# A fused attention, routing, experts and feed-forward kernel: attention loads run three groups ahead instead of eight, its two kinds of units alternate, and its rows are stored as they come

## The chip, the core and the metric

The kernel runs as one program on one NeuronCore of a Trainium2 chip. The metric is the time of one execution on the device, in microseconds; shorter is better. Five instruction streams run beside each other and wait for one another through semaphores: TensorE (PE; its weight loads are shown as PEld), VectorE (DVE), ScalarE (ACT), GpSimd (POOL) and SyncE (SP). SP computes nothing here: its stream issues DMAs. POOL issues DMAs too, besides some work of its own. All DMAs share the core's 16 DMA engines.

## What is computed

Attention over four batches, eight heads, 576 tokens and 64 features, in float32. Heads 0 to 3 see the last 32 tokens; heads 4 to 7 see the earlier tokens of the same residue modulo 32. The rows are then the input of a top-1 mixture of eight experts, and its result that of a feed-forward block with a squared ReLU:

```python
rel = pos[:, None] - pos[None, :]
mask_local = (rel >= 0) & (rel < stride)
mask_strided = (rel >= 0) & (pos[None, :] % stride == pos[:, None] % stride)
masks = np.stack([mask_local if h < H // 2 else mask_strided for h in range(H)], axis=0)
scores = np.where(masks[None], scale * (q @ k.transpose(0, 1, 3, 2)), -1e9)
attn = softmax(scores);  x = rows_of(attn @ v)              # (2304, 512)
...
logits = x @ w_gate + modality_bias[modality_id]
e_idx = np.argmax(logits, axis=1)                           # one expert a row
out[mask] = gate_w[mask, None] * (np.maximum(x[mask] @ w1[e], 0.0) @ w2[e])
...
r = np.maximum(x @ w_in, 0.0)
return (r * r) @ w_out
```

## The kernel before

**Stages.** `attention_and_routing` computes attention, stores its rows `xn` in the DRAM tensor `x1`, and works out which rows go to which expert. `moe_and_ffn` then gathers rows from `x1` by expert (the gathers wait for all stores), multiplies them by the experts' weights, and goes on to the feed-forward block. The change lies in the first stage alone.

**Units.** The list `units` holds 40 units of work: 22 strided ones (`"s"`, 108 rows each) and 18 local ones (`"l"`, 128 rows each). Before, all strided units come first (units 0 to 21), then all local ones (22 to 39). One turn of the loop over `k` is a software pipeline: SP gets the loads and stores of this turn; PE computes the scores of unit k into `sp` (L207), transposes the result of unit k-5 (`xq`, L317) and the weights of unit k-2 (`pp`, L236), and multiplies the weights of unit k-3 by v into `xp` (L253 for strided, L264 for local units). DVE takes the maximum, subtracts, and normalises unit k-5 into `xn`; ACT does the exponential and the copies out of PSUM. For every pair of rows' tiles that is complete (two local units, and the strided units that hold the same tokens), turns also carry the products with the gate's weights (`xq`, L358) and, a turn later, a short fold (`sp`, L369). `KEEP0` and `KEEP` add small matmuls on zeros (L192): four to two a turn in the first eleven turns, then one a strided unit and none a local one.

**Loads.** Units are loaded in groups: four of one strided unit, nine of two strided units, nine of two local units. A group has a tile `qk` and a tile `v`; each comes from a ring of `NLD` buffers, so a load waits until the group that held its buffer before has been used up (scores for `qk`, the product with v for `v`). `loads_to` issues them in order on SP; at turn k it goes as far as the group of unit k plus `NLD` - 1. Here `NLD` is 9. SP is in order: a load that waits holds up all DMAs behind it. It also waits, before each DMA, for the eighth one before it to land.

**Stores.** `store` writes one unit's `xn`: a local one as one DMA on SP (L302), a strided one as two or three on POOL (L310). `xn` has a ring of `NXN` = 15 buffers. Stores begin at turn `ST0` = 12, and those of local units wait until all loads have been issued.

**Other names.** `wg` and `fold` are the gate's weights and a small constant, loaded on SP (L403, L404) just ahead of the first load of a group of two. `N_LOC` is the number of tiles whose softmax of logits is done inside the loop. Line numbers here and in the rows are those of the kernel before.

Of the kernel before, what the change touches and what calls it, by code (L numbers as in the profile page):

```python
# [19 lines left out]
NE, FF, F2 = 8, 1024, 2048  # L20
STRIDE = 32
NJ = S // STRIDE
NTL = NT // 128
# [7 lines left out]
NST = -(-NT // SU)  # L31
# [9 lines left out]
NCV = 4  # L41
XR = 4
KEEP_R = (7, 9, 9)
NXN = 15
ST0 = 12
KEEP_D = 2
KEEP_X = 5
EARLY0 = (0, 0)
# [3 lines left out]
KEEP = {"s": 1, "l": 0}  # L52
KEEP0 = {0: 0, 1: 4, 2: 4, 3: 4, 4: 4, 5: 4, 6: 3, 7: 3, 8: 3, 9: 2, 10: 2}
NWM = 4
NLD = 9
NWS = 3
N_LOC = 8


@with_exitstack  # L60
# [25 lines left out]
def attention_and_routing(es, tc, a, x1, res):  # L86
    nc = tc.nc
    sy, ac, ve, gp, pe = nc.sync, nc.scalar, nc.vector, nc.gpsimd, nc.tensor
# [3 lines left out]
    cst = es.enter_context(tc.tile_pool(name="a_cst", bufs=1))  # L92
    ld = es.enter_context(tc.tile_pool(name="a_ld", bufs=NLD))
    wk = es.enter_context(tc.tile_pool(name="a_wk", bufs=3))
# [22 lines left out]
    wg = cst.tile([128, 4, 32], F32, name="wg")  # L117
    fold = cst.tile([128, NE], F32, name="fold")
# [4 lines left out]
    rt.warm = warm  # L123
    rt.spare = lambda: (bank("a0"), bank("a1"))

    units = [("s", t) for t in range(NST)] + [("l", t) for t in range(NTL)]
    NU = len(units)
    groups, gof = [], {}
    for kind, sizes in (("s", (1, 1, 1, 1) + (2,) * 9), ("l", (2,) * 9)):
# [29 lines left out]
    ngl = [0]  # L159

    def loads_to(k):
        while ngl[0] <= min(k, len(groups)):
            gi = ngl[0]
            if gi < len(groups):
                load_qk(gi)
            if gi > 0:
                load_v(gi - 1)
            ngl[0] += 1

    def geom(k):  # L170
        kind, t = units[k]
        gi, o = gof[kind, t]
        if kind == "s":
            return kind, t, 128 if t < NST - 1 else 64, 64, gi, o
        return kind, t, 128, 64, gi, o
# [6 lines left out]
    def stage_s(k):  # L182
        kind, t, n, w, gi, o = geom(k)
        sp = ps.tile([128, 2, 512], F32, tag="sp", name="sp")
        qk = qk_t[gi]
        if kind == "s":
            mk = mstr
        else:
            mk = mloc[:, 1 if (2 * t) % 9 == 0 else (2 if (2 * t + 1) % 9 == 0 else 0), :]
        mk = mk.unsqueeze(1).to_broadcast([128, 2, w])  # L190
        for i in range(KEEP0.get(k, KEEP[kind])):
            pe.matmul(sp[:, i % 2, 256:512], lhsT=warm[:, 0:128], rhs=warm[:, 0:256], start=True, stop=True)  # L192
        for par in range(2):
            pe.matmul(sp[:, par, 0:2 * w].rearrange("p (b w) -> p b w", b=2),
                      lhsT=identb, rhs=mk, start=True, stop=False, skip_group_check=True)
        for pr in range(2):
            for par in range(2):
                r0 = 64 * par
                if kind == "s":
                    cq, ck = (4 * o + pr) * SU, (4 * o + 2 + pr) * SU  # L200
                    blocks = [(g, cq + g * SR, m, ck + g * SR, m) for g, m in sgroups(t)]
                else:
                    cq, ck = 256 * pr + 128 * o, 512 + (256 + QB) * pr + 128 * o
                    blocks = [(j / 2, cq + QB * j, QB, ck + QB * j, 2 * QB) for j in range(4)]
                for g, cq, m, ck, mk_ in blocks:
                    p0 = int(64 * g)
                    pe.matmul(  # L207
                        sp[p0:p0 + m, par, pr * w:pr * w + mk_],
                        lhsT=qk[r0:r0 + 64, cq:cq + m],
                        rhs=qk[r0:r0 + 64, ck:ck + mk_],  # L210
                        start=False, stop=True, skip_group_check=True,
                    )
        st[k, "s"] = sp[0:n, :, 0:2 * w].rearrange("p a (b w) -> p a b w", b=2)
        return sp

    def v_max(k):
        kind, t, n, w, gi, o = geom(k)
        mx = wk.tile([128, 2, 2], F32, tag="mx", name="mx")
        ve.tensor_reduce(out=mx[0:n], in_=st[k, "s"], axis=AX.X, op=ALU.max)
        st[k, "m"] = mx  # L220

    def v_sub(k):
        kind, t, n, w, gi, o = geom(k)
        sm = wk.tile([128, 4 * w], F32, tag="sm", name="sm")
        sm4 = sm.rearrange("p (a b w) -> p a b w", a=2, b=2)[0:n]
        ve.tensor_tensor(out=sm4, in0=st.pop((k, "s")),
                         in1=st.pop((k, "m"))[0:n].unsqueeze(3).to_broadcast([n, 2, 2, w]), op=ALU.subtract)
        ac.activation(out=sm[0:n], in_=sm[0:n], func=AF.Exp, scale=scale)
        st[k, "p"] = sm

    def stage_t(k, pp=None):
        kind, t, n, w, gi, o = geom(k)
        p = st.pop((k, "p"))
        pp = bank("pp") if pp is None else pp
        for i in range(2):
            pe.transpose(pp[:, 128 * i:128 * i + n], p[0:n, 128 * i:128 * i + 128], ident[0:n, 0:n])  # L236
        pt = wk.tile([128, 2, 128], F32, tag="pt", name="pt")
        ac.activation(out=pt[:, :, 0:n], in_=pp.rearrange("p (h n) -> p h n", n=128)[:, 0:2, 0:n], func=AF.Copy)
        st[k, "t"] = pt
# [40 lines left out]
    def v_norm3(k):  # L280
        kind, t, n, w, gi, o = geom(k)
        xn = wk.tile([128, 256], F32, tag="xn", name="xn", bufs=NXN)
        ve.tensor_tensor(
# [12 lines left out]
    stores = []  # L296

    def store():
        k, xn = stores.pop(0)
        kind, t = geom(k)[0:2]  # L300
        if kind == "l":
            sy.dma_start(out=x1[t * 128:t * 128 + 128, 0:256], in_=xn)  # L302
        else:
            for g, rows in sgroups(t):
                c, p = 2 * t * CT + g * CT, 64 * g
                end = p + rows
                while p < end:
                    m = min((end - p) // NJ, STRIDE - c % STRIDE)
                    dst = x1.rearrange("(b j r) f -> b r j f", j=NJ, r=STRIDE)[c // STRIDE, c % STRIDE:c % STRIDE + m]
                    gp.dma_start(out=dst[:, :, 256:512], in_=xn[p:p + m * NJ])  # L310
                    c, p = c + m, p + m * NJ
# [54 lines left out]
    def folds(p, dst):  # L366
        t0, t1, lt = p
        for i in range(t1 - t0):
            pe.matmul(dst[:, NE * i:NE * i + NE], lhsT=lt[:, 128 * i:128 * i + 128], rhs=fold, start=True, stop=True)  # L369
        return t0, t1, dst[:, 0:NE * (t1 - t0)]  # L370
# [3 lines left out]
    def add(p):  # L374
        rt.add(*p)
        n_add[0] = p[1]

    def features(k):

        xq = bank("xq")  # L380
        t0 = lg_done[0]
        t1 = min(t0 + 2, lg_ready(max(0, k)))
        if t1 > t0 + 1:
            products(t0, t1, xq[:, 256:512])
        stage_x(k, xq)
        if t1 > t0 + 1:
            lt_p.append(fetch(t0, t1, xq[:, 256:512]))
            lg_done[0] = t1
# [11 lines left out]
    ngl[0] = 2  # L400
    loads_to(3)
    sy.dma_start(out=mloc, in_=a["mloc"])
    sy.dma_start(out=wg[:, :, 0:NE], in_=a["w_gate"].rearrange("(c p) e -> p c e", p=128))  # L403
    sy.dma_start(out=fold, in_=a["fold"])  # L404
    ac.activation(out=sc1, in_=sc1, func=AF.Exp)
    wu = bank("xp")
    for i in range(9):
# [5 lines left out]
    def side(n):  # L413
        while n and todo:
            if next(todo[0], todo) is todo:
                todo.pop(0)
            else:
                n -= 1

    def norm(u):  # L420
        v_norm1(u)
        v_norm2(u)
        v_norm3(u)

    loc = 0
    for k in range(NU):
        if k >= LN:
            norm(k - LN)
        side(1)
        loads_to(geom(k)[4] + NLD - 1)  # L430
        for _ in range(2):
            if k >= ST0 and len(stores) > 1 and (units[stores[0][0]][0] == "s" or ngl[0] > len(groups)):
                store()
        sp = stage_s(k)
        fd = folds(lt_p.pop(0), sp[:, 0, 192:256]) if lt_p else None
        v_max(k)
        if fd:
            add(fd)
        side(1)
        if k >= LX:  # L440
            features(k - LX)
        if k >= LT:
            stage_t(k - LT)
        side(1)
        v_sub(k)
        side(1)
        if k >= LV:
            stage_v(k - LV)
        if k == 3:
            rt.load_consts()  # L450
        if k == 8:
            rt.bias()
        if loc == 0 and n_add[0] >= N_LOC:
            todo += [rt.local(0, N_LOC), rt.gates(0, N_LOC)]
            loc = N_LOC

# [62 lines left out]
class Routing:  # L519
# [4 lines left out]
    def t_(self, shape, dt, name):  # L524
        return self.cst.tile(shape, dt, name=name)
# [88 lines left out]
    def finish(self):  # L614
# [19 lines left out]
        cb = t_([128, 2, 128], BF16, "cnb")  # L634
        gts = self.gates(N_LOC, T)
        next(gts)
# [1165 lines left out]
```

## Time and profile before

| | us |
|---|---|
| median of 3 runs (727.41 to 732.12) | 728.55 |
| the profiled execution | 728.09 |
| its span, first to last instruction | 726.3 |
| PE busy in the span | 702.6 (97%) |
| DVE, ACT, POOL busy | 516.6, 407.0, 151.6 |

The profiled execution lies 0.46 us under the median. A row of the span's slices has 40 digits, each the busy share of 18.2 us in tenths; PEclk is the clock that was granted to TensorE in the same tenths. The chain of waits runs backwards from the last instruction, at each step to what released it; "issue" in it is time in which the engine waited for nothing that the profile shows. The DMA queue called "instruction" carries the program itself to the engines, q1 carries what SP issues, q0 what POOL issues.

### The profile page before, as it was taken

To read this page: it belongs to the slowest core of one execution; us is meant where nothing else is said; L and a number is where in the kernel's file an instruction comes from. 1 tells how busy PE (TensorE), PEld (TensorE's weight loads), DVE (VectorE), ACT (ScalarE), POOL (GpSimd) and SP (SyncE) were. 2 spreads that over 40 slices of the span, in tenths; PEclk is the share of its full clock that TensorE was granted. 3 is DMA by queue.
4 is the path that set the end of the run, shared out by engine and by line. 5 is a ranking of instruction groups with operands and counts; after the bars stand their busy time and mean duration, and the time that the engine had idled before them with its cause. 6 is when DMAs were issued, how large, how long until landed. Compare 5 with 4: busy or idle time off the path is not lost.

```text
span 726.3 us, 15653 instructions
## 1 busy us (share of the span) xinstructions
PE 702.6 (97%) x6012; PEld 653.0 (90%) x6012; DVE 516.6 (71%) x1021; ACT 407.0 (56%) x791; POOL 151.6 (21%) x215
## 2 busy tenths in 40 slices
PE   8898997999999999999999999999999999999995
PEld 5665656999999989999999999999999999999995
DVE  5667776678868778775567899847747796773784
ACT  3455445545565466544566776657627746663761
POOL 7651013102320241021002444540000004000004
PEclk9879999999999999999999999999999999999998
DMA  8994118557686598455145799998887879878832
GB/s 257 390 382 156 59 39 264 202 191 230 232 288 196 175 312 304 159 176 216 38 163 166 272 333 357 366 323 256 250 247 247 256 234 328 254 247 245 258 90 88
DMA packets 69422, 167.90 MB, mean 231 GB/s; under 512 B 11064, under 2 KB 14552, under 8 KB 69344
## 3 DMA queue, kind: packets, MB, share of 16 engines
q1 hardware_dynamic: 53312, 125.14, 53.5%
q0 software_dynamic: 16032, 41.73, 16.0%
q8 instruction: 49, 0.80, 0.5%
q14 instruction: 29, 0.24, 0.1%
HBM read 128.00 MB, written 38.80 MB: 230 GB/s over the span
## 4 chain that ended last, share of the span: by engine, by line
PE 91%; DMA 2%; issue 2%; DVE 2%; POOL 1%; ACT 1%; SPq 0%; another core or an unknown queue 0%; POOLq 0%; ACTq 0%; DVEq 0%
PE hp L878 14%; PE yp L889 14%; PE fhp L1154 9%; PE op L1175 9%; PE lb L1472 7%; PE mb L1545 7%; PE md L1472 5%; PE la L1472 5%; PE md L1545 4%; PE ma L1545 4%; PE sp L207 2%; PE xq L317 2%; PE xp L253 1%; PE pp L236 1%; POOL out_dram L1182 1%
## 5 line engine op out<-in xcount | busy, mean ns | idle before, releaser
L848 DVE TENSOR_TENSOR w<-stg,w 128x1024 fp32r<-128x1024 f32 x56 | 68.4, 1223 | 43.1 <-ACT w L844 43.0
L844 ACT ACTIVATE w<-stg 128x1024 fp32r<-128x1024 f32 x56 | 59.2, 1059 | 70.3 <-PE yp L889 45.3
L878 PE MATMUL hp<-xh,w 128*128 128x384 f32 (+1 forms) x448 | 92.4, 328 | 1.9 <-ACT xh L870 0.7
L878 PEld LDWEIGHTS hp<-xh,w 128*128 128x128 f32 x448 | 76.7, 188 | 3.8 <-ACT w L844 1.3
L889 PE MATMUL yp<-hh,w 128*128 128x384 f32 x384 | 76.2, 340 | 0.0
L1154 PE MATMUL fhp<-xh,w 128*128 128x384 f32 x256 | 70.5, 336 | 0.0
L889 PEld LDWEIGHTS yp<-hh,w 128*128 128x128 f32 x384 | 66.9, 188 | 0.0
L1182 POOL DMA_INDIRECT out_dram<-x2t,idn x12 | 14.0, 1168 | 220.2 <-DVE x2t L1447 218.3
L1472 PE MATMUL lb<-xh,ws 128*128 128x384 f32 x192 | 55.0, 337 | 0.0
L1200 POOL DMA_DIRECT2D wd<-w x48 | 34.4, 897 | 88.5 <-DVE w L999 85.5
L1175 PE MATMUL op<-w,gh 128*128 128x512 f32 x192 | 49.1, 391 | 0.0
L1521 DVE TENSOR_TENSOR gl<-g,gh 128x384 fp32r<-128x384 f32 x64 | 33.5, 556 | 21.0 <-ACT gh L1520 21.0
L1154 PEld LDWEIGHTS fhp<-xh,w 128*128 128x128 f32 x256 | 46.7, 188 | 1.2
L878 PE MATMUL hp<-xl,w 128*128 128x384 f32 (+1 forms) x224 | 46.3, 328 | 0.0
L1154 PE MATMUL fhp<-xl,w 128*128 128x384 f32 x128 | 43.2, 338 | 0.0
L881 ACT ACTIVATE hh<-hp 128x384 fp32r<-128x384 f32 (+1 forms) x56 | 25.5, 456 | 31.1 <-PE hp L878 30.7
L1450 ACT ACTIVATE g<-g 128x384 f32<-128x384 f32 x48 | 25.1, 522 | 32.0 <-DVE g L1447 31.8
L1520 ACT ACTIVATE gh<-g 128x384 fp32r<-128x384 f32 x64 | 32.6, 523 | 16.4 <-PE mb L1545 8.2
L889 PE MATMUL yp<-hl,w 128*128 128x384 f32 x192 | 41.1, 336 | 0.0
L1175 PEld LDWEIGHTS op<-w,gh 128*128 128x128 f32 x192 | 35.6, 188 | 5.4
L878 PEld LDWEIGHTS hp<-xl,w 128*128 128x128 f32 x224 | 39.1, 188 | 0.0
L1545 PE MATMUL mb<-ws,gh 128*128 128x256 f32 x264 | 38.6, 282 | 0.5 <-ACT gh L1520 0.5
(299 smaller groups left out, 1723.1 us busy)
## 6 DMA issues: line engine op xcount, KB each, us to landing
ws<-wd SPq DMA_DIRECT2D x112, 512.0 KB, 4.5
stg<-in_wcat_dram SPq DMA_DIRECT2D x56, 512.0 KB, 4.0
stg<-in_w2cat_dram SPq DMA_DIRECT2D x32, 512.0 KB, 5.3
wd<-w POOLq DMA_DIRECT2D x48, 256.0 KB, 6.1
wd<-co POOLq DMA_DIRECT2D x16, 512.0 KB, 4.1
wd<-co POOLq DMA_DIRECT2D x32, 256.0 KB, 5.1
qk<-in_qkl_dram SPq DMA_DIRECT2D x9, 544.0 KB, 9.7
v<-in_vl_dram SPq DMA_DIRECT2D x9, 528.0 KB, 8.2
```

The costliest lines, as they stand in the source:

```text
L844: ac.activation(out=w[:, 0, :], in_=t, func=AF.Copy)
L848: ve.tensor_tensor(out=w[:, 1, :], in0=t, in1=w[:, 0, :].bitcast(F32), op=ALU.subtract)
L878: pe.matmul(hp, lhsT=w[:, wi, 128 * k:128 * k + 128], rhs=x[:, k, 0:n], start=(i == 0), stop=(i == 11))
L881: ac.activation(out=hh, in_=hp, func=AF.Relu)
L889: pe.matmul(yp[c][:, 0:SLOT], lhsT=w[:, wi, 512 + 128 * c:640 + 128 * c], rhs=x, start=(j == 0 and x is hh and wi == 0), stop=(j == NC1 - ...
L1154: pe.matmul(hp, lhsT=w[:, v, 128 * k:128 * k + 128], rhs=xs[ch, k // 2][xv][:, k % 2, :], start=(i == 0), stop=(i == 11))
L1175: pe.matmul(ops[ch][t], lhsT=x[:, 128 * t:128 * t + 128], rhs=w[:, v, :], start=(j == ORD[0] and first), stop=(j == ORD[-1] and last))
L1200: gp.dma_start(out=wd[lay, p // 4, 7 * (p % 4) + unit[lay][i]], in_=src)
L1472: pe.matmul(M[m], lhsT=w[:, v, k, :], rhs=xp_c[c][x][xv][:, k, :], start=(i < 3 and n == 0), stop=(n == 5), skip_group_check=True)
L1520: ac.activation(out=gh, in_=src, func=AF.Copy)
L1521: ve.tensor_tensor(out=gl, in0=src, in1=gh.bitcast(F32), op=ALU.subtract)
L1545: pe.matmul(at[t], lhsT=x[:, 128 * t:128 * t + 128], rhs=w[:, v], start=(new and e == 0 and x is gh and v == 0 and first), stop=(e == 3 an ...
```

## The change

Four constants and the list of units are changed. The list now has ten strided units, then local and strided ones by turns (`l0 s10 s11 l1 s12 l2 s13 l3 ...`, with two strided units in a row once), then the last seven local ones. Groups are sorted by their first unit as before, so groups of local and strided units also come by turns. `NLD` is 4: loads run three groups ahead. A store is issued as soon as a second one is pending, whatever its kind. `wg` and `fold` are loaded on POOL, in turn 3 behind the constants of the routing. `NXN` is 12, `N_LOC` 10.

```diff
-NXN = 15
-ST0 = 12
+NXN = 12
+S_FIRST = 10
+L_LAST = 7
...
-NLD = 9
+NLD = 4
...
-N_LOC = 8
+N_LOC = 10
...
-    units = [("s", t) for t in range(NST)] + [("l", t) for t in range(NTL)]
+    units = [("s", t) for t in range(S_FIRST)]
+    ns, nl = S_FIRST, 0
+    while ns < NST or nl < NTL - L_LAST:
+        if nl < NTL - L_LAST and (ns == NST or nl * (NST - S_FIRST) <= (ns - S_FIRST) * (NTL - L_LAST)):
+            units.append(("l", nl))
+            nl += 1
+        else:
+            units.append(("s", ns))
+            ns += 1
+    units += [("l", t) for t in range(nl, NTL)]
...
-    sy.dma_start(out=wg[:, :, 0:NE], in_=a["w_gate"].rearrange("(c p) e -> p c e", p=128))
-    sy.dma_start(out=fold, in_=a["fold"])
...
-            if k >= ST0 and len(stores) > 1 and (units[stores[0][0]][0] == "s" or ngl[0] > len(groups)):
+            if len(stores) > 1:
                 store()
...
         if k == 3:
             rt.load_consts()
+            gp.dma_start(out=wg[:, :, 0:NE], in_=a["w_gate"].rearrange("(c p) e -> p c e", p=128))
+            gp.dma_start(out=fold, in_=a["fold"])
```

SP's stream at the start, before; 128x432 is the `qk` of one strided unit, 128x864 that of a group of two:

```order
L154 DMA v<-in_vs_dram 128x264
L402 DMA mloc<-in_mloc_dram 128x192
L403 DMA wg<-in_w_gate_dram 128x4x8
L404 DMA fold<-in_fold_dram 128x8
L144 DMA qk<-in_qks_dram 128x864
L154 DMA v<-in_vs_dram 128x264
L144 DMA qk<-in_qks_dram 128x864
```

The same place in the change:

```order
L164 DMA v<-in_vs_dram 128x264
L412 DMA mloc<-in_mloc_dram 128x192
L154 DMA qk<-in_qks_dram 128x864
L164 DMA v<-in_vs_dram 128x264
L154 DMA qk<-in_qks_dram 128x864
```

Two DMAs ahead of the first load of a group of two have moved to POOL.

SP's stream late in the loads, before:

```order
L156 DMA v<-in_vl_dram 128x1056
L146 DMA qk<-in_qkl_dram 128x1088
L156 DMA v<-in_vl_dram 128x1056 x2
L302 DMA x_60<-xn 128x256 x18
L1006 TENSOR_LOAD regs
```

Late in the loads of the change:

```order
L156 DMA qk<-in_qkl_dram 128x1088
L164 DMA v<-in_vs_dram 128x528
L154 DMA qk<-in_qks_dram 128x864
L166 DMA v<-in_vl_dram 128x1056
L312 DMA x_60<-xn 128x256
L156 DMA qk<-in_qkl_dram 128x1088
L164 DMA v<-in_vs_dram 128x528
L312 DMA x_60<-xn 128x256
```

The 18 stores of local units, which stood behind all loads, now stand between loads, and loads of strided (`qks`, `vs`) and local groups (`qkl`, `vl`) alternate.

PE's stream in the middle of the stage, before, one turn:

```order
L207 MATMUL sp<-qk 54x54 x8
L317 MATMUL xq<-ident,xn 128x128 x2
L236 MATMUL pp<-ident,sm 128x128 x2
L253 MATMUL xp<-v,pt 64x65 x8
L192 LDWEIGHTS warm
L192 MATMUL sp<-warm 128x256
```

In the change, the score and value products of three turns in the middle:

```order
L217 MATMUL sp<-qk 32x64 x16
L327 MATMUL xq<-ident,xn 128x128 x2
L246 MATMUL pp<-ident,sm 128x128 x2
L263 MATMUL xp<-v,pt 64x65 x8
L202 LDWEIGHTS warm
L202 MATMUL sp<-warm 128x256
...
L217 MATMUL sp<-qk 54x54 x8
L327 MATMUL xq<-ident,xn 128x128 x2
L246 MATMUL pp<-ident,sm 128x128 x2
L274 MATMUL xp<-v,pt 32x65 x16
...
L217 MATMUL sp<-qk 32x64 x16
```

A local unit has twice as many score and value products (x16) as a strided one (x8); turns of both kinds now alternate, where ten strided turns and then eighteen local ones stood. PE has the same instructions in all but one more small matmul on zeros.

## Rows read from the trace of the kernel before

**Rows 1.** The page: TensorE's granted clock in 40 slices of 18.2 us.

```profile
PEclk9879999999999999999999999999999999999998
```

**Rows 2.** Windows of the attention stage: busy time by engine, granted clock, DMA share, GB/s.

```profile
10.00:57.00 47.00, 41.70 (x854) 30.53 (x852) 32.08 (x104) 22.55 (x84) 28.46 (x51) 0.85 1.04 376
57.00:90.00 33.00, 30.07 (x1086) 20.10 (x1084) 23.82 (x88) 16.81 (x52) 1.73 (x3) 1.00 0.28 91
```

**Rows 3.** Chain of waits, attention stage: start, duration, what; PE pieces begin a turn's scores.

```profile
6.96 5.09 DMA qk<-in_qks_dram
12.10 0.42 PE sp L207 x16
...
22.52 0.34 issue
...
25.40 0.35 PE sp L207 x16
...
27.06 0.35 PE sp L207 x16
...
28.37 1.90 issue
...
46.40 0.35 PE sp L207 x16
...
51.53 1.08 issue
...
57.04 0.39 issue
...
59.56 0.38 PE sp L207 x32
...
60.84 0.38 issue
...
61.79 0.39 PE sp L207 x32
...
63.37 0.38 PE sp L207 x32
64.57 0.57 issue
...
80.01 0.32 issue
...
84.22 0.50 issue
```

**Rows 4.** A fine window behind the longest stall; columns as in rows 2.

```profile
32.00:34.00 2.00, 2.00 (x37) 1.52 (x34) 1.43 (x5) 0.80 (x4) 1.45 (x3) 0.50 1.04 391
```

**Rows 5.** PE's waits, 4 to 100 us: total us, times, longest us.

```profile
PE xp L253 <- issue: 2.6, 3, 1.9
PE sp L207 <- DMA qk<-in_qks_dram: 2.0, 1, 2.0
PE sp L207 <- issue: 2.0, 3, 1.1
PE xp L264 <- issue: 1.7, 4, 0.6
```

**Rows 6.** DMA at 27 to 29 us: packets, MB, share; issues, KB, us to landing.

```profile
q8 instruction: 1, 0.02, 3.4%
...
qk<-in_qkl_dram SPq DMA_DIRECT2D x1, 544.0 KB, 10.5
```

**Rows 7.** The same at 46 to 51 us.

```profile
qk<-in_qkl_dram SPq DMA_DIRECT2D x2, 544.0 KB, 7.6
```

**Rows 8.** The same at 58 to 62 us.

```profile
q8 instruction: 1, 0.02, 1.8%
...
v<-in_vl_dram SPq DMA_DIRECT2D x1, 528.0 KB, 5.0
```

**Rows 9.** SP's timeline at the start: start us, duration, DMA.

```profile
5.99 0.38 SPq L403 DMA_DIRECT2D wg<-in_w_gate_dram  x1
```

## The prediction, made before the change had run

> **What bounds the kernel now.** I began with the granted clock in slices [rows 1]. It stands at 9 nearly throughout; the two low digits, 8 and 7, cover 18 to 54 us, inside the attention stage. The reader is to see that the only stretch in which TensorE is slowed lies where the change is made. Windows split the stage [rows 2]: up to 57 us the DMA engines are full (share 1.04, 376 GB/s) and the clock averages 0.85; from 57 to 90 us the share is 0.28 and the clock is whole. PE is busy for 89% and 91% of the two, so the stage is a string of turns on PE, and whatever lengthens a turn lengthens the kernel.
>
> The chain of waits then shows the turns as starts of score products [rows 3]. A strided turn at full clock takes 27.06 - 25.40 = 1.66 us, a local one 63.37 - 61.79 = 1.58. Between them stand pieces named "issue", in which PE waited for nothing that the profile shows: 0.34, 1.90 and 1.08 us while the DMA engines are full, 0.3 to 0.6 us later. Ten such waits make 2.6 + 2.0 + 1.7 = 6.3 us [rows 5]. They come at regular distances. From the end of one to the end of the next it is 65.14 - 61.22 = 3.92 us and 84.72 - 80.33 = 4.39 us in the quiet part, and 30.27 - 22.86 = 7.41 us in the full one [rows 3]. I read them as PE having run out of program: a packet of the instruction queue moves just before such a wait ends, and it takes as long when DMA is full (3.4% of 16 engines over 2 us, 1.1 us) as when it is quiet (1.8% over 4 us, 1.15 us) [rows 6, 8]. So what grows is the time before the packet starts. It grows with the depth of the queue: loads take 10.5 us to land where the refill took 7.4, 7.6 us ahead of the wait at 51.5, and 5.0 us where the refill takes 3.9 [rows 6 to 8].
>
> The longest wait costs twice. After it the clock is 0.50, the lower of the two levels (1.2 GHz) [rows 4]. From 27.06 to 46.40 us seven strided turns ran in 19.34 us where seven at 1.66 make 11.62 [rows 3]. That is 7.7 us, the largest loss in the stage.
>
> **The change, part by part.**
>
> *Start.* PE waits 2.0 us for the load that was issued at 6.96 us and took 5.09 us to land [rows 3, 5]. Now the loads of `wg` and `fold` no longer stand ahead of it on SP; its slot is that of `wg`, 5.99 us [rows 9], 0.97 us earlier. Its new condition, that the scores of unit 0 are done so that their buffer is free, is met by then, since a turn's score products take 0.42 us and begin as soon as the first loads land. Those two loads are many small pieces and no longer move ahead of it either, so it may land sooner still. Bounds: 0.97 and the whole wait, 1.97; I take 1.5. On POOL the two loads stand before stores that have turns to spare, and nothing needs `wg` before turn 19.
>
> *Depth of the queue.* With four buffers, and from turn 10 on two groups in use at once, two groups at most are on their way: 2 x (544 + 528) KB = 2.2 MB, at 376 GB/s 5.8 us, and mostly one, 2 to 3 us of transfer. That is the depth at 58 to 62 us or at 46 to 51 us [rows 7, 8], not that at 27 us. So a refill should take 3.9 to 4.8 us (4.8 is 57.43 - 52.61, from the end of the wait at 51.53 to the end of the next [rows 3]) instead of 7.4.
>
> *What a refill may take.* PE lives on one block for 28.37 - 22.86 = 5.51 us in strided turns, 64.57 - 61.22 = 3.35 us in local ones, and 84.22 - 80.33 = 3.89 us in local ones with gate products [rows 3]. A strided and a local turn by turns use 1.66/5.51 + 1.58/3.35 = 0.77 of a block in 3.24 us: 4.2 us a block, about 4.5 with gate products. Against refills of 3.9 to 4.8 us that leaves waits of 0 to 0.6 us, where strided turns alone would have none at all.
>
> *The sum.* (1) Start: -1.5. (2) The wait at 22.52 goes: -0.34, and the pipeline's restart behind each wait, (61.79 - 59.56) - 1.58 - 0.38 = 0.27 us [rows 3]: -0.6. (3) The 1.90 us wait and the halved clock go: -7.7. (4) The wait at 51.53: -1.08 - 0.27 = -1.35. (5) The other seven waits are 6.3 - 3.3 = 3.0 us, with restarts 4.9. In their place come about 13 refills from turn 12 on (the same program over the same turns: some 50 us at about 4 us a block): four in the last seven local turns, which stay as they are at 0.4 + 0.27, 2.7 us; nine in the mixed turns at 0.18 + 0.27, 4.1 us. Together 6.8: +1.9. (6) One more matmul on zeros: +0.15. The sum is -9.1 us.
>
> *What I cost at nothing.* Gate products, folds, score and value products are the same in number and only move. Loads ahead: each load is issued at least five turns before its use, 8.1 us at 1.6 us a turn, against a landing of 5 to 7.6 us. Local stores now stand between loads on SP and wait for `xn` of a unit one turn back; behind them stand loads that still have four to five turns. Rows end being stored after the last turn, as before, so the gathers wait for the same thing. DVE and ACT have the same work; if PE's waits vanish, DVE is late next, with 32.08 us busy in 47 and 23.82 in 33 [rows 2]. The larger `N_LOC` takes two tiles out of a chain of small operations at the end; I give it nothing. Everything from the gathers on has the same instructions and starts earlier by the same amount.
>
> Against its own execution (728.09 us, 0.46 under the median) the change gives 728.1 - 9.1 = **719.0 us**. The case's own range: with 1.97, no mixed waits and the rest, 714.5; with 0.97, the wait at 22.5 kept, and 1.27 us for each of nine refills, 727.5.
>
> **The rivals.**
>
> *A: a second fall of the clock.* Some wait in the mixed turns is again long enough. For it: in the mixed part DMA is busy for much longer than now, up to 90 us. Against: the wait of 1.08 us did not bring the clock down, and I expect none above that. Price: 19.34 - 11.62 - 1.90 - 0.27 = 5.5 us, so 724.5. Chance 0.10.
>
> *B: the waits have nothing to do with the queue*, and the change does not do what I read from it. They would recur at the same places in the program, the clock would fall as before, and only the start is gained: 726.6 us. Against: 7.41 us against 3.92 for the same packet. The Trainium skill ("Runtime: NRT & Kernel Launch", section "Instruction fetch mechanics") says that crossing from one block of the program to the next is mostly hidden. Here the trace does not agree: ten waits without a releaser, 6.3 us [rows 5]. Chance 0.08.
>
> *C: slower. Refills wait behind any busy queue, not a deep one.* Then what counts is how long loads are on the move, and the change stretches that over all mixed turns, in which a block also lasts 4.2 to 4.5 us and no longer 5.5. Four mixed units load and store 2.3 MB, 6.1 us at 376 GB/s, in 6.5 to 8 us of turns. Were the nine refills to take 7.4 us where they meet loads, and about half do, they cost 9 x 0.5 x 3.3 = 15 us where I have 4.1, that is 730; where all do, or the clock falls as well, up to 745. I price the case at 735. It decides from a mean refill of 5.5 us: each microsecond beyond the 4.5 assumed costs 9. Against it: the block behind the wait at 51.5 took 4.8 us under a DMA still full. The Trainium skill ("DMA: Bandwidth & Descriptors", section "Queues, rings and completion order") says that a DMA engine goes round the queues that have work, a packet at a time. By that rule a refill would wait for a packet and never for a depth, busy queues would all delay it alike, and the gain would not come. The growth with landing time [rows 6 to 8] speaks against it. Chance 0.13.
>
> *D: loads come late*, since strided and local groups share four buffers and SP is held up by its first waiting load. At a landing of 10.5 us each later group would be 2.4 us late, some 15 us over the six that matter, so 734. Chance 0.05.
>
> **The numbers.** The forecast has 0.64. A run tells about 1% (7.3 us) from no change. Of the forecast's cases about four in five lie below 721.3: faster 0.51. Its rest (0.13), A, B and the mild end of C and D (0.03) make no change: 0.34. The rest of C and D: slower, 0.15. The range of 714 to 732 us takes in the case's own 714.5 to 727.5, A, B and the mild end of C.
>
> **What would show it.** Right: no stretch at clock 0.50 before 57 us; "issue" waits under 1.1 us, a block every 4 to 4.8 us in the mixed turns; loads that land in 4 to 7 us; the last turn of attention and the first expert's products some nine us earlier than before. Wrong: "issue" waits of 2 us and more between 25 and 70 us, a clock of 0.50 there, or PE waiting for `qk` or `v` in the mixed turns.

## The result, and the profile after

The change makes the kernel slower: 736.74 us (735.29 to 737.91) against 728.53 us of the kernel before, a ratio of 1.0105, 95% interval [1.0071, 1.0138]. A second measurement of the same kernel, beside another set of runs of the kernel before, gave 734.74 us, 1.0085 [1.0052, 1.0118]. The forecast was 719.0 us, and the range ended at 732: both time and sign were wrong. The profiled execution took 737.09 us, its span is 735.3 us.

The row of the granted clock answers to [rows 1]. It is below 9 in four digits where two stood, from 37 to 110 us, and lowest in the fifth (74 to 92 us), at the end of attention:

```profile
PEclk9988689999999999999999999999999999999999
```

Windows of the attention stage (PE, PEld, DVE, ACT, POOL busy; granted clock, DMA share, GB/s) answer to [rows 2]:

```profile
10.00:34.00 24.00, 22.71 (x582) 16.87 (x586) 19.72 (x65) 13.56 (x50) 18.89 (x34) 1.00 0.97 318
34.00:57.00 23.00, 19.16 (x493) 13.30 (x486) 12.98 (x43) 9.90 (x35) 6.06 (x11) 0.83 0.72 226
57.00:90.00 33.00, 29.70 (x775) 20.15 (x774) 20.90 (x72) 14.93 (x50) 6.65 (x11) 0.81 0.73 226
```

Up to 34 us the clock is whole, and the DMA engines move 318 GB/s, still busy for 0.97 of the time. But from 57 to 90 us, which was quiet (share 0.28, clock 1.00), DMA is busy for 0.73 of the time and the clock is 0.81.

The chain of waits (start, duration, what), pieces that answer to [rows 3]:

```profile
5.99 4.57 DMA qk<-in_qks_dram
10.61 0.42 PE sp L217 x16
...
25.29 1.14 issue
...
34.79 1.98 issue
...
50.84 1.86 issue
...
63.99 0.44 issue
...
73.61 0.90 issue
...
78.03 1.96 issue
...
93.01 0.58 PE sp L217 x32
```

The fifth turn, which waited for its load, begins at 10.61 us in place of 12.10: the start's gain of 1.5 us is there. The wait at 28.37 and its fall of the clock are gone. In their place stand three waits of nearly two microseconds each, 1.98, 1.86 and 1.96 us, the last of them in local turns, where 0.3 us stood at 80 us. The last turn's scores start at 93.01; before it was 89.38. PE's waits from 4 to 95 us, in all (us, times, longest), answer to [rows 5]:

```profile
PE sp L217 <- issue: 3.6, 3, 2.0
PE xp L274 <- issue: 2.9, 2, 2.0
PE xp L263 <- issue: 1.9, 1, 1.9
```

They make 8.4 us (8.3 by the pieces of the chain) where 6.3 stood; nothing there waits for a load but once, for 0.2 us. Each of the three long waits is followed by the lower clock level, as [rows 4] showed for one; the shorter ones are not. Windows laid on these stretches:

```profile
38.80:42.20 3.40, 3.40 (x82) 2.06 (x78) 2.22 (x7) 1.07 (x3) 1.21 (x2) 0.50 0.70 241
52.50:59.30 6.80, 6.60 (x119) 4.93 (x123) 3.31 (x11) 1.77 (x6) 1.21 (x2) 0.50 0.63 159
79.80:93.40 13.60, 13.42 (x314) 8.68 (x314) 8.04 (x33) 4.56 (x15) 0.62 (x1) 0.50 0.34 95
```

That is 23.8 us at 1.2 GHz; before it was one stretch of 13.6 us:

```profile
31.80:45.40 13.60, 13.60 (x196) 9.88 (x195) 8.14 (x27) 5.70 (x21) 8.23 (x14) 0.50 1.04 392
```

The DMA view from 23.9 to 77.5 us (packets, MB, share; for issues KB and us to landing) answers to [rows 6 to 8]:

```profile
q8 instruction: 10, 0.16, 1.2%
...
qk<-in_qkl_dram SPq DMA_DIRECT2D x7, 544.0 KB, 5.0
v<-in_vl_dram SPq DMA_DIRECT2D x7, 528.0 KB, 5.5
```

Loads land in 5.0 and 5.5 us, as forecast for the shallower queue. Ten packets of program, 16 KB each, moved in these 53.6 us. Take off the waits in them (1.14 + 1.98 + 1.86 + 0.44 + 0.90 = 6.3 us) and what 10.2 us at half clock cost (4.1 us, by the price of 0.40 us a microsecond that is worked out below the table of all kernels). Then a block of program lasted 4.3 us, as forecast too (4.2 to 4.5).

**Where the time went.** The last turn starts 3.6 us later. The first expert's products, first before and then in the change, start 5.3 us later:

```profile
119.86 6.54 PE hp L878 x36
125.17 6.51 PE hp L888 x36
```

1.7 us of this arise between the last turn and these products, in the routing's end and the gathers. Two stretches of 3.4 us at half clock lie there, at 103.7 and 113.9 us; the profile of the kernel before has none between 95 and 120 us. The other 3.5 us of the profiled difference arise in the run of the eighth expert's weights (a wait of 7.85 us for a load into `stg`). A second profile of the same kernel (experiment `again`) does not have them, so they do not belong to every execution of the change.

### The profile page after: what moved, and what is told of

Same layout as the page of the kernel before. It is cut to its first block, busy times and chain, and to the rows that moved or that the text cites. A ratio compares the mean times of both kernels' runs of the same rounds, so it can differ in the third digit from the quotient of the medians.

```text
span 735.3 us, 15665 instructions
## 1 busy us (share of the span) xinstructions
PE 710.5 (97%) x6013; PEld 657.5 (89%) x6013; DVE 516.9 (70%) x1021; ACT 407.5 (55%) x791; POOL 152.8 (21%) x217
## 4 chain that ended last, share of the span: by engine, by line
PE 89%; DMA 3%; DVE 2%; issue 2%; POOL 1%; ACT 1%; SPq 1%; POOLq 0%; ACTq 0%; DVEq 0%
PE hp L888 14%; PE yp L899 13%; PE fhp L1164 9%; PE op L1185 9%; PE lb L1482 7%; PE mb L1555 6%; PE md L1482 5%; PE la L1482 5%; PE md L1555 4%; PE ma L1555 4%; PE sp L217 2%; PE xq L327 2%; DMA stg<-in_wcat_dram 2%; PE pp L246 1%; PE xp L263 1%
## 5 line engine op out<-in xcount | busy, mean ns | idle before, releaser
L888 PEld LDWEIGHTS hp<-xh,w 128*128 128x128 f32 x448 | 77.5, 190 | 5.8 <-ACT w L854 3.5
```

Of the source, the lines that this page charges most:

```text
L888: pe.matmul(hp, lhsT=w[:, wi, 128 * k:128 * k + 128], rhs=x[:, k, 0:n], start=(i == 0), stop=(i == 11))
```

## The experiments

The theory, called "busy" in the expectations: a refill of PE's program is delayed by whatever traffic the DMA engines carry, by an amount that varies from one refill to the next; put traffic into turns whose blocks last 3.4 to 4.5 us, and some refills outlast their block by 1.4 to 2.5 us; such waits bring the clock down. The main rival is the prediction's own reading: only a deep queue delays a refill, and something else in the change costs the time (the order of units, four buffers, the stores). All ratios are to runs of the kernel before on the same chip, with 95% intervals.

**Fewer buffers alone (`n4`).** The kernel before with

```diff
-NLD = 9
+NLD = 4
```

> The kernel before with four load buffers instead of nine, and nothing else changed. Theory 'busy' (a refill of PE's program is delayed by any loads on the move, however few; what counts is how short PE's blocks are while loads move): the loads of the local groups now move during local turns, whose blocks last 3.35 us; waits of 1 to 3 us there, the clock at 0.50 for a good part of the local turns; strided turns with few waits. 733 to 745 us. Theory 'deep' (the prediction's: only a deep queue delays a refill): waits of at most 0.6 us, no stretch at 0.50; 719 to 723 us. Theory 'turns' (the alternation itself slows PE): order as before, so 728 or less.

Measured: 727.16 us, 0.9989 [0.9965, 1.0013]. The theory, which had asked for 733 to 745 us, missed here, and so did the reading by depth (719 to 723 us). The chain has these waits, among others, up to 60 us:

```profile
27.52 0.56 issue
...
33.66 1.20 issue
...
45.17 1.91 issue
...
51.50 0.67 issue
...
55.57 0.93 issue
```

Waits of 1.2 us (in a strided turn) and 1.9 us (in the first local turn) stand here although loads land in 4.7 to 4.8 us. The second was not followed by a fall (the windows up to 57 us show a clock of 1.00); a later one of 1.38 us was. So fewer buffers alone cost nothing that can be measured, and they do not remove the waits either. What the theory had left out is a gain: the refill in turn 12, behind which PE waited 1.90 us before [rows 3], now makes a wait of 0.56 us, and no fall follows. The profile has 6.8 us at half clock in attention in place of 13.6, though the local turns now carry loads (DMA share 0.62 from 57 to 90 us, before 0.28).

**The order of units of before, with all else of the change (`seq`).**

```diff
-S_FIRST = 10
+S_FIRST = 22
...
-N_LOC = 10
+N_LOC = 8
```

> The change with its units in the order of before (all strided ones first, and the routing's 8 tiles in the loop); four buffers, stores as they come and the two small loads on POOL stay. 'busy': as with four buffers alone less the 1.5 us of the start, 731 to 743 us, with the long waits in the local turns. 'deep': 718 to 722. 'turns': 8 to 10 us less than the change, 727 to 729, without the three stretches at half clock.

Measured: 729.96 us, 1.0035 [0.9998, 1.0072]. Without the alternation most of the loss is gone. The time lies just below the range of the theory (731 to 743 us) and just above that of 'turns' (727 to 729 us). Its interval reaches into both, so this run does not decide between them.

**The alternation with nine buffers (`t9`), and with six (`t6`).** The change with

```diff
-NLD = 4
+NLD = 9
```

and, for `t6`, 6.

> The change with nine load buffers instead of four; order, stores and the rest as in the change. 'busy': loads end early again, at about 55 to 60 us; until then the mixed turns' blocks of 4.2 us meet full queues, waits of 2 to 3 us there and the clock falls, then quiet turns with waits of 0 to 0.4 us; 727 to 736. 'deep': worse than the change, 740 or more, since the queue is deepest where blocks are short. 'turns': as the change, 735 to 738.

> The change with six load buffers: between the change (four, 736.7) and nine (730.2). 'busy': loads end earlier than with four and later than with nine, so 731 to 734, with one or two falls of the clock in the mixed turns. If the cost of four buffers is SP being held up by its first waiting load, six remove it: 728 to 730.

Measured: 730.23 us, 1.0043 [1.001, 1.0076], and 732.81 us, 1.0055 [1.0018, 1.0091]. With the change's four buffers that makes a series: 1.0043, 1.0055, 1.0085 to 1.0105. The later the loads, the more of them fall into mixed and local turns (DMA share from 57 to 90 us 0.34, 0.62, 0.73), and the slower; nine and six buffers are not apart by their intervals. Neither the alternation with nine buffers nor four buffers in the old order was measured to cost more than some 3 us; together they cost 5.6 to 8.2. The reading by depth had asked for 740 us or more of `t9`, 'turns' for 735 to 738: both missed. The share does not settle the time alone: it is 0.62 in `t6` (1.0055) and in `n4` (0.9989).

**Traffic added to the kernel before (`busy`).** Eleven loads of 500 KB that nobody reads, in turns 26 to 36:

```diff
+        if 26 <= k <= 36:
+            dum = ld.tile([128, 1000], F32, tag="dum", name="dum", bufs=2)
+            sy.dma_start(out=dum, in_=a["qkl"][:, 0, 0:1000])
```

> The kernel before with one more load of 500 KB in each of the turns 26 to 36, into a tile that nothing reads (two buffers, so that few are on the move at once). The local turns, quiet before, get DMA traffic at some 0.8 of the engines' time with a shallow queue, landing in 3 to 5 us. 'busy': refills there take 5 to 6 us instead of 3.9, waits grow from 0.3 to 0.6 us to 1 to 2.5 us each, and the clock falls to 0.50 at least once; 733 to 742 us. 'deep': refills 3.9 to 4.4 us as before, waits unchanged; 728 to 730. 'turns' says nothing: 728.

Measured: 736.56 us, 1.0146 [1.0112, 1.018]. The four times, 735.25 to 738.66 us, lie above all 21 of the kernel before (724.97 to 731.37). Two windows and the waits of the chain:

```profile
57.00:90.00 33.00, 29.48 (x895) 19.31 (x885) 19.05 (x64) 13.47 (x41) 2.22 (x4) 0.79 0.80 249
70.70:77.50 6.80, 6.80 (x152) 4.29 (x152) 3.19 (x11) 2.30 (x7) 0.00 (x0) 0.50 0.76 244
```

```profile
27.27 1.90 issue
...
47.69 1.63 issue
...
68.66 1.65 issue
...
83.77 1.85 issue
```

PE's work, the order and the buffers are those of before. The added loads are issued from 56.8 to 85.7 us; the first two waits, and the falls behind them, come before that and are not theirs. (The second fall lasts to 63.9 us and lowers the clock of the wide window.) With a share of 0.80 in place of 0.28, waits of 1.65 and 1.85 us stand in local turns where the longest was 0.6 [rows 5]; behind the first of them the clock is at half for 6.8 us, behind the second it does not fall. Two such loads at most are on their way at once: traffic through a short queue is enough. One profile places only some 3 us of the loss with the added loads. The clocks of all runs say more: 0.972 to 0.976 over the span, on average 0.974, against 0.975 to 0.994, on average 0.984, in the 21 runs of before. That is some 14.5 us more at half clock, 5.8 us by the price below.

**Traffic taken out of the change (`thin`).** All local units use the first local group's tiles; the other eight groups are not loaded. Its local rows are therefore those of wrong tokens. Strided groups and the one local group also get rings of their own, with four buffers and one.

```diff
+        if kind == "l" and t0:
+            qk_t[gi] = qk_t[gof["l", 0][0]]
+            return
...
+        if kind == "l" and t0:
+            v_t[gi] = v_t[gof["l", 0][0]]
+            return
```

> The change, but all local units read the first local group's tiles, so that eight of the nine local groups are not loaded (8.8 MB of 17.7 MB of loads) and PE's program is the same. What this leaves out: the local rows are those of wrong tokens, so the routing and the later stages may differ in length; only the attention stage is to be read. 'busy': with little on the move in the mixed turns a refill takes 3.6 to 4.4 us against blocks of 4.2 to 4.5: waits of at most 0.5 us, no stretch at half clock from turn 12 on, the last scores at 79 to 83 us instead of 93.3. 'turns' (alternation itself is slow, whatever the loads): waits of other kinds stay, the last scores at 88 us or later.

Measured: 719.74 us, 0.9874 [0.985, 0.9898]. That this is near the 719.0 us forecast for the change is chance: the change loads eight groups more. The later stages are not shorter for the wrong rows: from the first expert's products (112.07 us) to those of the feed-forward block it takes 223.2 us, counted from first record to first record, in the kernel before 223.4.

```profile
57.00:90.00 33.00, 32.09 (x953) 21.67 (x951) 24.95 (x94) 18.48 (x58) 5.47 (x10) 1.00 0.24 71
```

```profile
25.65 1.53 issue
...
40.02 0.83 issue
...
45.66 0.48 issue
...
55.07 0.40 issue
```

The order of units, PE's instructions and the stores are the change's. Without the traffic, waits after the first one, behind which the clock falls for 3.4 us, stay under 0.9 us. The clock is whole from 34 us to the end of attention, and the last turn starts at 80.36 us, 12.7 us earlier than in the change. So the alternation of units costs nothing by itself.

**The start alone (`wg`), and with four buffers (`n4wg`).** `wg` and `fold` are loaded on POOL in turn 3, all else as before; the second also has `NLD` 4.

```diff
-    sy.dma_start(out=wg[:, :, 0:NE], in_=a["w_gate"].rearrange("(c p) e -> p c e", p=128))
-    sy.dma_start(out=fold, in_=a["fold"])
...
+            gp.dma_start(out=wg[:, :, 0:NE], in_=a["w_gate"].rearrange("(c p) e -> p c e", p=128))
+            gp.dma_start(out=fold, in_=a["fold"])
```

> The kernel before with only the two small loads moved from SP to POOL. PE's first wait shortens by 1.0 to 1.97 us; all else as before: 726 to 727.5 by the prediction's first term. If the start is given back in the next refill wait: 728.

> The kernel before with four load buffers and the two small loads on POOL: what the change has without the alternation and without its stores. 'busy': as with four buffers alone less 1 to 1.5 us, 725.5 to 726.5, and 3 to 4 us less than the change in the order of before (730.0), whose stores of local rows move among the local loads. If those stores cost nothing: 729 to 730.

Measured: 728.85 us, 1.0002 [0.9964, 1.0041], and 728.3 us, 0.998 [0.9952, 1.0009]. The fifth turn comes earlier (the load is issued at 5.93 us and takes 4.87), but none of it reaches the end: in `wg` the last turn starts at 89.68 us, before at 89.38, after two waits of 1.90 and 1.63 us with a fall behind each. That fits the expectation of a start that is given back (728 us), not the 726 to 727.5 us of the prediction's first term. The gain of `n4wg` is within its measurement; the theory had asked for 725.5 to 726.5 us and missed.

**Six buffers in the order of before (`n6`).**

> The kernel before with NLD 6 and nothing else, between 9 (728.5) and 4 (727.2). 'busy': the strided turns, whose blocks last 5.5 us, still carry most of the loads; waits of 1.4 to 1.9 us once or twice, 7 to 14 us at half clock, 726 to 729 us. The rival 'depth' (only a deep queue delays a refill): with less of a queue than before the wait at 28 us goes and none takes its place: 720 to 723 us.

Measured: 728.63 us, 0.9982 [0.995, 1.0014]. A shallower queue does not bring the 720 to 723 us that the reading by depth asks for; the time is within the theory's 726 to 729. The profiled execution is the slowest of the ten, 736.92 us. After one wait of 1.90 us in turn 12 its clock is at half for 41.0 us, with PE busy throughout, where the theory had expected 7 to 14 us.

**The change again (`again`).**

> The change itself, unaltered, for a second profiled execution. Theory 'busy' (DMA traffic in turns whose program blocks last 3.4 to 4.5 us delays some refills past the block; the waits of 1.4 us and more bring the clock down): again waits of 1.4 to 2.5 us in the mixed turns, 15 to 28 us at half clock before 95 us, last scores at 92 to 95 us, 735 to 738 us in all. If the first execution's three long waits were chance, the last scores come at 88 to 91 us. The 3.5 us that were lost between the first expert's products and the first ones of the feed-forward block, in a wait for a load into stg: if the change causes them, that stretch is 226 to 228 us again; if they are chance, it lies between 222 and 225 us, as in the other kernels, and part of the median's 8.2 us stays without a place.

Measured: 734.74 us, as said. Waits of the chain, and windows on the stretches at half clock:

```profile
25.33 1.53 issue
...
39.75 2.35 issue
...
63.56 2.38 issue
...
82.17 1.71 issue
...
91.90 0.91 issue
...
93.81 0.61 PE sp L217 x32
```

```profile
27.90:31.30 3.40, 3.40 (x91) 2.17 (x85) 2.21 (x9) 1.80 (x7) 2.52 (x5) 0.50 0.94 285
41.50:51.80 10.30, 9.70 (x148) 6.46 (x148) 4.40 (x15) 3.57 (x12) 1.20 (x2) 0.50 0.55 149
65.40:75.70 10.30, 9.76 (x197) 6.76 (x196) 5.30 (x17) 3.32 (x10) 1.20 (x2) 0.50 0.70 209
```

A fourth fall begins at 92.7 us, behind the wait at 91.90; behind that at 82.17 there is none. Which refills are late, and which waits bring the clock down, differs from one execution to the next; in all it is five waits of 8.9 us where the first profile has six of 8.3. The last turn comes 0.8 us later than in the first profile, the first expert's products (125.07) 0.1 us earlier. From there to the first products of the feed-forward block it takes 348.68 - 125.07 = 223.6 us, in the kernel before 343.42 - 119.86 = 223.6.

**All kernels side by side**: PE's waits without a releaser from 4 to 95 us (sums of rounded rows), the granted clock from 10 to 95 us and the DMA share from 57 to 90 us by windows, and the start of the last turn's scores.

| kernel | ratio | waits, us | clock | share | last turn |
|---|---|---|---|---|---|
| before | 1 | 6.3 | 0.92 | 0.28 | 89.38 |
| change | 1.0105 | 8.4 | 0.86 | 0.73 | 93.01 |
| change, again | 1.0085 | 8.9 | 0.85 | 0.74 | 93.81 |
| n4 | 0.9989 | 8.2 | 0.96 | 0.62 | 87.80 |
| seq | 1.0035 | 7.7 | 0.92 | 0.63 | 88.91 |
| t9 | 1.0043 | 6.3 | 0.88 | 0.34 | 90.07 |
| t6 | 1.0055 | 7.9 | 0.88 | 0.62 | 92.05 |
| busy | 1.0146 | 7.0 | 0.84 | 0.80 | 94.12 |
| thin | 0.9874 | 3.3 | 0.98 | 0.24 | 80.36 |
| wg | 1.0002 | 4.2 | 0.84 | 0.25 | 89.68 |
| n4wg | 0.9980 | 6.7 | 0.90 | 0.63 | 89.53 |
| n6 (its slowest execution) | 0.9982 | 3.5 | 0.76 | 0.61 | 95.81 |

A mean clock of 0.92 over 85 us is 2 x 0.08 x 85 = 13.6 us at half. One microsecond at half clock costs 0.40 us: the 5.5 us that the prediction worked out for its 13.6 us [rows 3]. Take a kernel's waits and this cost off the start of its last turn, and 74.6 to 77.6 us are left in all twelve rows, where the starts themselves lie 15 us apart. So two things decide the stage in each of these kernels, waits for program and the clock behind them; the order of the units is not needed as a third.

That these waits are for program the prediction had read off the packets. The places bear it out. Counted in matmuls and weight loads on record, the waits of before stand ahead of PE's 692nd, 942nd, 1692nd, 1942nd, 2194th, 2448th and so on: one or more steps of 250 to 256 apart, at the ends of blocks. In the other kernels with the old order they stand at the same counts within two, and in those with units by turns at such steps too (944th, 1448th, 2204th, 2710th in the change). The program fixes where PE can run dry; only the length of each wait changes.

No version with the reference's work beats the kernel before: the intervals of `n4`, `n4wg` and `n6` hold 1.

## Why the prediction was wrong

- **Start (term 1): right.** 12.10 - 10.61 = 1.49 us against 1.5. But `wg` shows that this alone moves nothing at the end.
- **The long wait and its fall (term 3): right at its place, but the gain was not kept.** At 28 us neither is left. In the old order the queue's depth does tell at this refill, ahead of the 942nd instruction. With nine or six buffers the wait is 1.90 us every time (kernel before, `wg`, `busy`, `n6`), with a fall behind it; with four it is 0.56 us (`n4`), 0.25 us (`seq`) or absent (`n4wg`), with none. Around it loads land in 7.3 to 10.3 us in the first four and in 4.1 to 5.5 us in the others; the DMA share from 20 to 30 us is 1.04 to 1.07 and still 0.93 to 1.00. But with four buffers a wait of 1.8 to 2.4 us comes ten turns later, where 1.08 us stood before. And with units by turns the depth does not tell at the same refill (944th): 1.26 us with nine buffers, 1.53 with six, 1.14 and 1.53 with four. So depth is one cause of a late refill, not the only one.
- **The other waits (term 5): the step that failed**: "Against refills of 3.9 to 4.8 us that leaves waits of 0 to 0.6 us". The block was right (4.3 us), and so was the landing of loads. But the bounds of the refills came from three examples, 3.92 and 4.39 us in quiet turns and 4.8 us behind the wait at 51.53, and the working of the 0.18 us a refill in the sum is not given. The refill from 74.52 us (end of one wait) to 79.99 (end of the next) took 5.5 us. Those that ended the waits at 34.79 and 50.84 took about 4.3 + 1.9 = 6.2 us, an estimate from the mean block. About half of the refills took less than their block and cost nothing. A wait is what a refill takes beyond its block and never less than nothing, so the late ones cost and the early ones give nothing back. The waits came to 8.3 us where the sum had 9 x 0.18 + 4 x 0.4 = 3.2: 5.1 us too few. Six restarts in place of 13 take off 1.9.
- **No fall of the clock**: the sum had none in the mixed turns; there were 23.8 us of it, 9.5 us at 0.40. With these three the forecast of -9.1 becomes -9.1 + 5.1 - 1.9 + 9.5 = +3.6 us; the last turn came 3.6 us late. The clock is the larger part in this pair of executions. In the medians it need not be: the profile of before has a mean clock of 0.987 over its span, while 13 runs of the same kernel beside `again` had 0.980 on average, and the four runs of `again` 0.978. By the price of 0.40 that is 1.3 of the 5.1 us between the two averages. How the rest divides between waits and what follows attention, runs without a profile do not tell.
- **Rival A** (a second fall, 0.10) was this mechanism, priced for one fall; there were three. "I expect none above that" rested on the waits of term 5.
- **Rival B**: false as it stood. The waits do come at fixed places in the program, but their length goes with the loads: with the traffic taken out (`thin`) they go from 8.4 to 3.3 us.
- **Rival C** (refills wait behind any busy queue, 735 us, 0.13) had the direction and, in the main, the cause: `busy` and `thin` show that traffic counts without a deep queue. That its time came out is luck in part: it had 15 us of waits and no fall, the trace has 2 us more of waits and 4 us more of the fall. Whether the mean refill reached its 5.5 us cannot be read, since a refill is seen to end only where PE waits for it; ten packets came 5.4 us apart with all waits and slow clock in between. By the Trainium skill ("DMA: Bandwidth & Descriptors", section "Queues, rings and completion order") a DMA engine goes round the queues that have work, a packet at a time; by that rule alone depth would not count. The waits in `busy` agree with it; those at the 942nd instruction (1.90 us with a deep queue, at most 0.56 with a short one) do not. What sets one refill's delay stays open.
- **Rival D** (late loads): false; PE waited 0.2 us for a load.
- The costs set at nothing hold as far as seen: `seq`, which has the stores between loads, four buffers and the shorter ring of `xn`, was measured at 1.0035, by its interval at most 1.0072.

What stays open: the 5.3 us at the first expert's products are about the loss of the second measurement (5.6 us). Of the first one's 8.2 us the profile places the rest in one execution's wait for `stg`, which did not come back, though the other three runs of that set are as slow. Nor is it settled why the same traffic in local turns cost nothing in the old order (`n4`, `n4wg`: share 0.62 and 0.63).

## What to carry to other kernels

Where an engine runs out of program, set the whole spread of refills against the length of a block, not a few examples of it, and ask which turns have the short blocks: loads that are moved into those turns can cost more than the queue they leave. Price a wait on PE with the clock that may fall behind it, and where the longest wait is removed, look for the next place with as much traffic before its gain is counted. Traffic is best tried directly: a kernel with dummy loads and one with loads left out told more here than those that moved the same loads about.

## What had not been expected of the hardware

In eleven profiles of attention (all but `n6`), 22 of 26 waits for program of 1.38 us or more had the granted clock go to 0.50 between 0.6 us before their end and 2.0 us after it; of 14 waits between 0.8 and 1.3 us only two. It then stayed there for 3.4 to 13.7 us though PE was busy for nearly all of it (13.42 of 13.60 us); in `n6` it stayed for 41.0 us. The falls also go, loosely, with the spread from run to run of one and the same kernel: of 25 runs of the kernel before on one chip, those at the ends took 725.87 us at a mean clock of 0.980 and 735.09 us at 0.965, of 21 on another 724.97 us at 0.994 and 731.37 us at 0.979. In between other things count as well: two runs on the first chip took 725.87 and 728.89 us at the same 0.980. The wait of 1.97 us at the start, for a load, had no fall behind it [rows 1, 5]; why that is, no run here tells.
